# Queries and keys of a pair of heads: two transfers with a buffer each in place of one

## Chip, core and metric

The kernel runs on one NeuronCore of a Trainium2 chip. The metric is the device time of one execution in microseconds (us). Engines: PE multiplies matrices, DVE and ACT work on vectors, POOL hardly takes part, SP issues all transfers (DMAs).

## What is computed

Two parts, one after the other. First, attention over 8 batches of 8 heads (head dimension 64): 32 global tokens that see all 544 tokens, and 512 local tokens that see the global ones and a band of 32 to either side. Then a feed-forward layer on the 4352 tokens of 512 features. The reference, cut:

```python
def _attn_ref(q_l, k_l, v_l, q_g, k_g, v_g):
    s_g = scale * np.matmul(q_g, k_all.transpose(0, 1, 3, 2))
    out_g = np.matmul(sm(s_g), v_all)
    s_ll = np.where(np.abs(pos[:, None] - pos[None, :]) <= 32, scale * q_l @ k_l^T, -1e9)
    a_l = sm(np.concatenate([scale * q_l @ k_g^T, s_ll], axis=-1))
    out_l = np.matmul(a_l, np.concatenate([v_g, v_l], axis=2))
    return np.concatenate([out_g, out_l], axis=2)

def _moe_ref(x, w_in, w_out):          # x: all heads of a token side by side
    h = x @ w_in                        # 512 -> 2048
    sp = np.maximum(h, 0.0) + np.log1p(np.exp(-np.abs(h)))
    return (h * erf(sp)) @ w_out        # 2048 -> 512
```

All products are in float32: an operand is split into a high and a low part, and three products of parts are summed (names that end in h and l).

## The kernel before

**Attention.** The function `attention(b, h, key)` (line 480) records the operations of one head; heads come in pairs that share the loads of queries and keys. Of a pair, Q is 128 x 544 and K is 128 x 768 words (K holds the blocks of keys in the order in which the windows of 128 keys need them). From the second batch on both are one tensor `qk` in HBM and one buffer `QK` of two in the pool, with `View`s on the two parts (lines 489 to 491):

```python
QK = abuf([P, SQ + NENT * WB], f"qk_{nm}", "qk", 2)
Q, K = View(QK, lambda t: t[:, :SQ]), View(QK, lambda t: t[:, SQ:])
held_by = [QK]
```

and one load brings them (line 510). The first batch has separate buffers and loads already, in memory that serves the weights later (table `EARLY`, line 63). The scores `s` of a pair read Q and K; DVE masks them and finds maxima (`sm`, `mx`), ACT takes exponentials, PE transposes (`t`), ACT or DVE copies (`pt`), PE multiplies with the values `va` and `vb` (`o`), and the normalised rows go by `xn` and `xT` to a buffer `xsc` in HBM. The global tokens have the products `ga`, `gb`, `gt`, `go`, `gx`.

**Feed-forward.** A chunk is one batch of 512 local tokens; the ninth holds the global ones. Output weights are brought, converted on ACT and DVE and split (`raw_out`, `top_out`, `wouth`, `woutl`); three units of 256 features each are resident. Names such as `op_0_5_3` read: half 0 of the features, chunk 5, tile 3. For chunks 0 to 5 and 8, the first half is computed between the heads (`h`, then `sp`, `gh`, `gl`, then the projection `op`). The rest uses a two-level scheme with seven products for a pair of chunks (function `products`, line 1316; banks `pa`, `pb`, `pc`, `pd`), whose operands are blocks and sums of blocks of the chunks (function `pair_blocks`, line 1260; B11, T1, T2, B21, B22, T3, T4 from loads `rx`). The product pa needs B11, pb needs T2.

**The order of the work** is not written out. Every operation is recorded with the engines that may take it, an estimated duration and a key; `Program.schedule` (line 192) then plays the program through with a model of engines and transfers, takes at each moment the ready operation of the smallest key (products of one kind are kept together by `NEAR`), and the instructions are issued in the order it finds. SP's queue is one of the engines of that model, so all transfers stand in one order, and a transfer that waits for a buffer holds up those behind it. The keys come from some hundred numbers at the head of the file (`HKEYS`, `HOFF`, `QLEAD`, `WOUT`, `GA1` and others). In the views all operations have the lines of a few helpers: 398 and 399 for PE, 400 and 401 for ACT, 402 for transfers, 410 for DVE.

Of the kernel before, what the change touches and what calls it, by code (L numbers as in the profile page):

```python
# [12 lines left out]
F32 = mybir.dt.float32  # L13
# [9 lines left out]
P = 128  # L23
# [6 lines left out]
FIRSTU = 3  # L30
CROWD, STRETCH, EVADE = 254, 4.013, 0.444
LOADED = (8.0, 36.0, 5.5)
# [7 lines left out]
GOFF, POFF = 10.828, 3.328  # L40
WIN, WOUT = (4.562, -0.85, -2.097), (8.325, 8.046, 8.583)
BIASED, AG = 30, 3
SHARED = (-99.0, -3.776)
TPAIR = 4.07
KEEP, KSTEP, FIRST = 23.915, 0.995, (11.832, 24.33)
CVO = (28.333, 40.99, 63.455, 72.447, 78.297)
QLEAD2, XDEL, SLOTS = 4.703, -1.599, 11
GATE1, GATE2, PROJ1, PROJ2 = (23.641, 17.389, 19.913), (24.543, 35.77, 36.437), 20.101, 32.087
SPT = 0.35
BIAS, AHEAD = 1.451, 14.561  # L50

# [15 lines left out]
EARLY |= {f"vb_0_{h}": ("xh" if h % 2 == 0 else "xl", 3) for h in range(6)}  # L67
WLEAD = 2.692
LATER, GFIRST = 8, (-3.958, -8.992)
HOFF = (-0.395, -0.257, -0.438, -0.817, -0.264, -0.516, -0.398, -1.043, -0.725, 0.706, 1.098, 1.046, 1.486, -0.653, 2.583, -0.948, 0.685, -0.013, 0.188, 0.75, 0.727, 0.252, 0.107, -0.027, -0.444, -0.245, 0.179, 0.265, 4.756, -1.498, 3.211, 2.883)  # L70
XOFF = (11.098, -2.917, 1.105, 8.898, 3.5, -3.863, -28.764, 5.954, 2.659)
UOFF = (2.338, -0.165, -2.537, -3.201, 2.006, 5.153, 52.335, -8.177, -3.667)
GFF = (-1.126, -0.376, -2.083, -1.393, -3.192, -14.288, -5.04, -1.158, -9.133)
PFF = (-3.459, 0.743, -4.102, 3.348, 5.735, 1.295, -10.989, -6.661, 15.971)
KQ = (-1.903, 0.178, 5.248, 31.079, 26.846, -19.85, -36.139, 22.153, 100.464, 4.644)
NORMAL = 1.125 * 2.0**-15
STRAIGHT, XLATE = True, -0.456
NS = 1
CSLAG = -20.54
KIN = (15.525, 30.452, 26.054)  # L80
GA1, GA2, PA1, PA2 = (1.398, 1.139, 20.144), (20.415, 21.216), 12.862, 17.045
AOFF = (5.616, 3.312, -17.499, -6.93)
XDELA = (2.207, -33.316, -10.264, -7.382)
LOFF = (3.06, 3.64)
_TUNE = ("KIN", "GA1", "GA2", "PA1", "PA2", "AOFF", "XDELA", "LOFF", "CSLAG")
# [28 lines left out]
class View:


    def __init__(self, whole, cut):
        self.whole, self.cut = whole, cut

    @property  # L120
    def ap(self):
        return self.cut(self.whole.ap)

# [236 lines left out]
def kernel(  # L360
    ctx: ExitStack,
    tc: tile.TileContext,
    qk: bass.AP,
    vA: bass.AP,
# [6 lines left out]
    nc = tc.nc  # L371
    B, NPAIR, _, SQ = qk.shape
    SQ -= NENT * WB
    H = 2 * NPAIR
# [105 lines left out]
    def attention(b, h, key):  # L480
        nm = f"{b}_{h}"
        p, r0 = h // 2, (h % 2) * D
        if h % 2 == 0:
            parts = qk[b, p][:, :SQ], qk[b, p][:, SQ:]
            if f"k_{nm}" in EARLY:
                Q, K = abuf([P, SQ], f"q_{nm}", "q", 2), abuf([P, NENT * WB], f"k_{nm}", "k", 2)
                held_by = [Q, K]
            else:
                QK = abuf([P, SQ + NENT * WB], f"qk_{nm}", "qk", 2)
                Q, K = View(QK, lambda t: t[:, :SQ]), View(QK, lambda t: t[:, SQ:])  # L490
                held_by = [QK]
            st["now"] = Q, K, held_by
            if NH * b + h == 0:
                add({"SP": 0.01}, key - QLEAD - 0.01, lambda: None, [], [Q, K])
                for n, (q0, q1, k0, k1) in enumerate(((0, 288, 0, 416), (288, SQ, 416, NENT * WB))):
                    for j, (t, src, c0, c1) in enumerate(((Q, parts[0], q0, q1), (K, parts[1], k0, k1))):
                        PIECE[n, j] = fixed(None)
                        add(
                            {"SP": SPT},
                            key - QLEAD,  # L500
                            lambda t=t, src=src, c0=c0, c1=c1: dma(t.ap[:, c0:c1], src[:, c0:c1]),
                            [t],
                            [PIECE[n, j]],
                            moved=0.512 * (c1 - c0),
                        )
# [7 lines left out]
        (Q, K, held_by), XN = st["now"], st["xn"]  # L513
        VA = abuf([P, NENT // 4, D + 1], f"va_{nm}", "va", 5)
# [6 lines left out]
        if h % 2 == 0:  # L521
# [16 lines left out]
            if NH * b + h == 0:  # L538
                PIECE[2, 0] = fixed(None)
                for n in range(2):  # L540
                    need = [Q, K, PIECE[n, 0], PIECE[n, 1]]
                    add(
                        {"PE": 0.55},
                        key,
                        lambda n=n: scores(range(2 * n, 2 * n + 2)),
                        need + SS * n,
                        [PIECE[2, 0]] if n else SS,
                        heat=1024,
                        ins=64,
                        mode="S",  # L550
                    )
            elif h % 4 == 2 and b >= GSJOIN:
                GA, GB, more = global_scores(b, h // 4, [st["qk", 0], (Q, K, held_by)])
# [6 lines left out]
                add({"PE": 1.9}, key, joint, [*st["qk", 0][2], *held_by], [*SS, GA, GB, GTURN], heat=3136, ins=160, mode="S")  # L560
# [188 lines left out]
    def global_scores(b, j, qk):  # L749
# [817 lines left out]
```

## Time and profile before

| | us |
|---|---|
| median of 3 runs | 897.86 (897.18 to 898.85) |
| profiled execution | 901.88 |
| its span, first to last instruction | 900.1 |
| PE busy | 882.4 |
| DVE busy | 688.3 |
| ACT busy | 549.8 |
| mean granted clock of PE | 0.996 |

The page comes from one profiled execution. Its span runs from the first to the last instruction; the execution's own time is 1.78 us longer. A duration on PE is that of a matmul from its start to a modelled end, and matmuls overlap; the distance of two starts is the better price of one. An engine's idle time is charged to what ended it; "issue" means that the engine waited for nothing that the profile shows.

### The profile page before, as it was taken

What the parts mean: (1) busy time and instruction counts of PE and PEld (TensorE: products, weight loads), DVE (VectorE), ACT (ScalarE), POOL (GpSimd) and SP (SyncE); (2) the same over time, 40 slices, a digit from 0 to 9 for tenths busy, and PEclk for the clock granted to TensorE, in tenths of its full rate; (3) what the DMA queues carried; (4) which work ended last, traced back from release to release, by engine and by line L of the source; (5) the groups of instructions that cost most, each with busy time, mean ns of one, the idle gap of its engine ahead of it and who ended that gap; (6) DMA issues with size and microseconds to landing.
All of it is one profiled execution on the core that took longest, in us unless ns stands there. A gap on an engine that the chain in (4) does not pass through costs nothing.

```text
span 900.1 us, 22151 instructions
## 1 busy us (share of the span) xinstructions
PE 882.4 (98%) x8781; PEld 717.2 (80%) x8789; DVE 688.3 (76%) x1839; ACT 549.8 (61%) x948; POOL 0.9 (0%) x5
## 2 busy tenths in 40 slices
PE   8899899999999999999999999999999999999998
PEld 4677777777877888888888888888888888888986
DVE  6898998999999978978598987587555956456443
ACT  5588866885588746854564865456524654455660
POOL 0000000000000000000000000000000000000000
PEclk9999999999999999999999999999999999999999
DMA  9898798799788948368676528444393435435222
GB/s 322 293 294 293 267 301 301 257 306 320 265 273 286 313 132 281 105 239 277 213 249 202 178 69 269 164 119 151 108 279 102 134 114 176 146 93 171 75 78 70
DMA packets 120063, 186.43 MB, mean 207 GB/s; under 512 B 14104, under 2 KB 57624, under 8 KB 119960
## 3 DMA queue, kind: packets, MB, share of 16 engines
q1 hardware_dynamic: 119960, 185.02, 62.9%
q8 instruction: 69, 1.13, 0.5%
q14 instruction: 34, 0.28, 0.1%
HBM read 143.56 MB, written 41.42 MB: 206 GB/s over the span
## 4 chain that ended last, share of the span: by engine, by line
PE 88%; DVE 6%; DMA 2%; issue 2%; ACT 1%; SPq 1%; DVEq 0%; ACTq 0%
PE op L398 40%; PE h L398 10%; PE pd L398 7%; PE pc L398 7%; PE pa L398 7%; PE pb L398 3%; PE o L398 3%; PE t L399 3%; PE s L398 3%; DVE sm L410 2%; PE h_g L398 2%; PE gt L399 1%; PE go L398 1%; PE ga L398 1%; DMA k<-in_qk_dram 1%
## 5 line engine op out<-in xcount | busy, mean ns | idle before, releaser
L398 PE MATMUL op<-wouth,gh 128*128 128x512 f32 x544 | 214.8, 395 | 0.0
L398 PE MATMUL op<-wouth,gl 128*128 128x512 f32 x544 | 211.9, 390 | 0.0
L398 PE MATMUL op<-woutl,gh 128*128 128x512 f32 x544 | 211.9, 389 | 0.0
L401 ACT ACT_TABLE_LOAD x105 | 134.7, 1283 | 2.6 <-PEq L1554 0.7
L398 PEld LDWEIGHTS op<-wouth,gh 128*128 128x128 f32 x544 | 102.1, 188 | 21.5 <-issue 0.6
L398 PEld LDWEIGHTS op<-wouth,gl 128*128 128x128 f32 x544 | 102.1, 188 | 21.5
L398 PEld LDWEIGHTS op<-woutl,gh 128*128 128x128 f32 x544 | 102.2, 188 | 20.0
L410 DVE TENSOR_TENSOR gl<-sp,gh 128x512 fp32r<-128x512 f32 x136 | 91.2, 685 | 19.6 <-PE op L398 16.0
L400 ACT ACTIVATE gh<-sp 128x512 fp32r<-128x512 f32 x67 | 42.0, 631 | 100.7 <-PE op L398 91.4
L400 ACT ACTIVATE sp<-sp 128x512 f32<-128x512 f32 x136 | 76.0, 621 | 0.5
L410 DVE CAST gh<-sp 128x512 fp32r<-128x512 f32 x69 | 28.6, 421 | 55.3 <-PE op L398 54.9
L410 DVE CUSTOM_DVE_ANT_0 sm<-s,msk 128x128 f32<-128x128 f32 x256 | 57.1, 285 | 17.3 <-PE s L398 17.2
L398 PE MATMUL h<-xh,winh 128*128 128x512 f32 (+1 forms) x168 | 67.0, 399 | 0.0
L398 PE MATMUL pa<-xh_x_B,wq 128*128 128x512 f32 x184 | 63.9, 389 | 0.0
L398 PE MATMUL pd<-xh_ih_T,wq 128*128 128x512 f32 x184 | 63.8, 389 | 0.0
L398 PE MATMUL h<-xh,winl 128*128 128x512 f32 (+1 forms) x168 | 63.2, 376 | 0.0
L398 PE MATMUL h<-xl,winh 128*128 128x512 f32 (+1 forms) x168 | 63.1, 376 | 0.0
L410 DVE TENSOR_TENSOR pair<-u,pc 128x512 f32<-128x512 f32 x46 | 31.4, 683 | 32.9 <-PE pc L398 32.8
L400 ACT ACTIVATE sm<-sm,mx 128x128 f32<-128x128 f32 x120 | 37.4, 394 | 9.1 <-DVE mx L410 9.1
L399 PE MATMUL t<-cs,sm 128*128 128x128 f32 x256 | 39.2, 286 | 3.0 <-DVE rs L410 1.1
L398 PE MATMUL o<-va,pt 128*32 128x65 f32 x768 | 37.8, 222 | 4.2 <-issue 3.5
L400 ACT ACTIVATE pt<-t 128x512 f32<-128x512 f32 x52 | 30.0, 600 | 17.8 <-PE t L399 17.7
(160 smaller groups left out, 1687.9 us busy)
## 6 DMA issues: line engine op xcount, KB each, us to landing
wq<-wq SPq DMA_DIRECT2D x161, 256.0 KB, 3.4
vb<-in_vB_dram SPq DMA_DIRECT2D x64, 325.0 KB, 5.6
qk<-in_qk_dram SPq DMA_DIRECT2D x28, 656.0 KB, 5.9
rx<-xsc SPq DMA_DIRECT2D x26, 512.0 KB, 6.0
va<-in_vA_dram SPq DMA_DIRECT2D x64, 195.0 KB, 5.3
wq<-part SPq DMA_DIRECT2D x47, 256.0 KB, 4.5
part<-os SPq DMA_DIRECT2D x34, 256.0 KB, 3.3
os<-part SPq DMA_DIRECT2D x34, 256.0 KB, 4.2
```

What stands on the lines that cost most here:

```text
L398: pe = lambda n, *a, **k: pinned(nc.tensor.matmul(n, *a, **k))
L399: tr = lambda *a, **k: pinned(nc.tensor.transpose(*a, **k))
L400: act = lambda *a, **k: pinned(nc.scalar.activation(*a, **k))
L401: table = lambda name: pinned(nc.scalar.preload_act_table_set(name))
L410: return lambda *a, **k: pinned(f(*a, **k))
```

## The change

Queries and keys are two tensors in HBM (`qT`, `kE`). Every pair has a buffer Q and a buffer K, two of each in the pool, and two loads with the same key, queries first. The class `View` that cut a buffer in two is gone (a helper class that was called `Whole` now bears its name). The numbers that set the order have other values. The diff, cut (of the tables of numbers a few lines stand for all):

```diff
-CROWD, STRETCH, EVADE = 254, 4.013, 0.444
+CROWD, STRETCH, EVADE = 254, 4.013, 0.627
...
-HKEYS = ((0, -5.932), (11, -0.913), (22, 0.765), (64, 30.197))
-STEP, GKEY = 0.093, -1.339
-QLEAD, VLEAD, RLEAD, XLEAD = 0.027, -1.614, -0.422, 4.406
+HKEYS = ((0, -5.577), (11, -1.054), (22, 0.793), (64, 30.035))
+STEP, GKEY = 0.091, -1.319
+QLEAD, VLEAD, RLEAD, XLEAD = -0.05, -1.622, 0.29, 4.309
...
-NEAR = 3.364
+NEAR = 2.617
...
-            parts = qk[b, p][:, :SQ], qk[b, p][:, SQ:]
-            if f"k_{nm}" in EARLY:
-                Q, K = abuf([P, SQ], f"q_{nm}", "q", 2), abuf([P, NENT * WB], f"k_{nm}", "k", 2)
-                held_by = [Q, K]
-            else:
-                QK = abuf([P, SQ + NENT * WB], f"qk_{nm}", "qk", 2)
-                Q, K = View(QK, lambda t: t[:, :SQ]), View(QK, lambda t: t[:, SQ:])
-                held_by = [QK]
-            st["now"] = Q, K, held_by
+            st["q"] = Q = abuf([P, SQ], f"q_{nm}", "q", 2)
+            st["k"] = K = abuf([P, NENT * WB], f"k_{nm}", "k", 2)
...
-            elif len(held_by) == 2:
-                load(key - QLEAD, Q, parts[0], 278)
-                load(key - QLEAD, K, parts[1], 393)
             else:
-                load(key - QLEAD, QK, qk[b, p], 671)
-            st["qk", p % 2] = st["now"]
+                load(key - QLEAD, Q, qT[b, p], 278)
+                load(key - QLEAD, K, kE[b, p], 393)
+            st["qk", p % 2] = (Q, K)
...
-                add({"PE": 1.02}, key, scores, held_by, SS, heat=2048, ins=128, mode="S")
+                add({"PE": 1.02}, key, scores, [Q, K], SS, heat=2048, ins=128, mode="S")
...
-_INS = ["qk", "vA", "vB", "cst", "w_in", "w_out"]
+_INS = ["qT", "kE", "vA", "vB", "cst", "w_in", "w_out"]
...
-    return dict(qk=np.concatenate([qT, kE], axis=3), vA=vA, vB=vB, cst=cst, w_in=wi, w_out=wo)
+    return dict(qT=qT, kE=kE, vA=vA, vB=vB, cst=cst, w_in=wi, w_out=wo)
```

The order of the instructions moves with it. Three places follow, with the numbers of the buffers (the last number of a name only counts buffers; `qk_2_0` is the pair of heads 0 and 1 of batch 2).

SP, the loads of the first two pairs of batch 2, before:

```order
L402 DMA xsg_88<-gxT_1_0_1260 128x2x32
L402 DMA qk_2_0_1324<-in_qk_dram 128x1312
L402 DMA qk_2_2_1334<-in_qk_dram 128x1312
L402 DMA vb_1_7_1409<-in_vB_dram 128x650
L402 DMA vb_1_4_1424<-in_vB_dram 128x650
```

and in the changed kernel:

```order
L391 DMA xsg_88<-gxT_1_0_1268 128x2x32
L391 DMA q_2_0_1332<-in_qT_dram 128x544
L391 DMA k_2_0_1334<-in_kE_dram 128x768
L391 DMA q_2_2_1344<-in_qT_dram 128x544
L391 DMA k_2_2_1361<-in_kE_dram 128x768
L391 DMA vb_1_7_1421<-in_vB_dram 128x650
L391 DMA vb_1_4_1436<-in_vB_dram 128x650
```

Each load is cut in two, keys directly behind their queries, and the rest keeps its order. It is so for most pairs; in the whole program SP has 654 transfers in place of 626.

SP, the first two pairs of batch 3, before:

```order
L402 DMA qk_3_2_2058<-in_qk_dram 128x1312
L402 DMA xsc2_82<-xT_2_1_2032 128x512
L402 DMA qk_3_0_2076<-in_qk_dram 128x1312
L402 DMA vb_2_4_2133<-in_vB_dram 128x650
L402 DMA vb_2_5_2156<-in_vB_dram 128x650
L402 DMA va_2_7_2162<-in_vA_dram 128x390
L402 DMA va_3_2_2194<-in_vA_dram 128x390
```

and in the changed kernel:

```order
L391 DMA q_3_2_2074<-in_qT_dram 128x544
L391 DMA xsc2_82<-xT_2_1_2048 128x512
L391 DMA k_3_2_2092<-in_kE_dram 128x768
L391 DMA q_3_0_2139<-in_qT_dram 128x544
L391 DMA vb_2_4_2172<-in_vB_dram 128x650
L391 DMA vb_2_5_2178<-in_vB_dram 128x650
L391 DMA k_3_0_2189<-in_kE_dram 128x768
L391 DMA va_2_7_2196<-in_vA_dram 128x390
L391 DMA va_3_2_2221<-in_vA_dram 128x390
```

Here the keys come later than their queries: one store, or two loads of values, lie between.

PE, the hand-over from attention to the two-level products, where pa and pb of the first unit begin, before:

```order
L398 MATMUL op_0_5_3_7090<-woutl_0_1_1444,gh_0_5_3_7117 128x512
L398 MATMUL op_0_5_3_7090<-wouth_0_1_1079,gl_0_5_3_7132 128x512
L398 MATMUL pa_0_3_0_7226<-xh_x0_3_B11_7009,wq0_0_3_0_6788 128x512
L398 MATMUL pa_0_3_0_7226<-xl_x1_3_B11_7043,wq0_0_3_0_6788 128x512
L398 MATMUL pa_0_3_0_7226<-xh_x0_3_B11_7009,wq0_0_3_0_6788 128x512 x2
L398 MATMUL pa_0_3_0_7226<-xl_x1_3_B11_7043,wq0_0_3_0_6788 128x512
L398 MATMUL pa_0_3_0_7226<-xh_x0_3_B11_7009,wq0_0_3_0_6788 128x512
L398 MATMUL pb_0_3_0_7239<-xh_x2_3_T2_7129,wq4_0_3_0_6798 128x512
L398 MATMUL pb_0_3_0_7239<-xl_x3_3_T2_7155,wq4_0_3_0_6798 128x512
```

and in the changed kernel:

```order
L387 MATMUL op_0_4_3_7067<-woutl_0_1_2373,gh_0_4_3_6822 128x512
L387 MATMUL op_0_4_3_7067<-wouth_0_1_1933,gl_0_4_3_6829 128x512
L387 MATMUL pa_0_3_0_7111<-xh_x0_3_B11_7004,wq0_0_3_0_6839 128x512
L387 MATMUL pa_0_3_0_7111<-xl_x1_3_B11_7021,wq0_0_3_0_6839 128x512
L387 MATMUL pa_0_3_0_7111<-xh_x0_3_B11_7004,wq0_0_3_0_6839 128x512 x2
L387 MATMUL pa_0_3_0_7111<-xl_x1_3_B11_7021,wq0_0_3_0_6839 128x512
L387 MATMUL pa_0_3_0_7111<-xh_x0_3_B11_7004,wq0_0_3_0_6839 128x512
L387 MATMUL op_0_4_2_7041<-wouth_0_2_1085,gh_0_4_4_6737 128x512
L387 MATMUL op_0_4_2_7041<-woutl_0_2_1456,gh_0_4_4_6737 128x512
```

The product pa stood at row 2543 of PE's order and stands at 2471; behind it 24 projection matmuls of chunks 4 and 5 now come before pb, which followed it directly.

DVE at the same place, up to the low part of block T2, before:

```order
L410 TENSOR_TENSOR rt_0_3_7060<-rx_0_7_0_6884,rx_0_6_0_6862 128x1024
L410 TENSOR_TENSOR woutl_1_1_7034<-top_out_1_1_1_6978,wouth_1_1_6903 128x512
L410 TENSOR_TENSOR rx_0_7_0_6884<-rx_0_7_1_6931,rx_0_7_0_6884 128x1024
L410 TENSOR_TENSOR xl_il0_3_B22_7087<-rx_0_7_1_6931,xh_ih0_3_B22_7073 128x512 x2
L410 TENSOR_TENSOR xl_x7_3_T1_7100<-rt_0_3_7060,xh_x6_3_T1_7084 128x512 x2
L410 CAST gh_0_5_2_7112<-sp_0_5_2_6703 128x512
L410 TENSOR_TENSOR rt_0_3_7060<-rx_0_7_1_6931,rt_0_3_7060 128x1024
L410 TENSOR_TENSOR gl_0_5_2_7121<-sp_0_5_2_6703,gh_0_5_2_7112 128x512
L410 TENSOR_TENSOR gl_0_5_3_7132<-sp_0_5_3_6915,gh_0_5_3_7117 128x512
L410 TENSOR_TENSOR gl_0_5_4_7134<-sp_0_5_4_6916,gh_0_5_4_7114 128x512
L410 TENSOR_TENSOR gl_0_5_5_7153<-sp_0_5_5_6917,gh_0_5_5_7119 128x512
L410 TENSOR_TENSOR xl_x3_3_T2_7155<-rt_0_3_7060,xh_x2_3_T2_7129 128x512 x2
```

and in the changed kernel:

```order
L399 TENSOR_TENSOR gl_0_5_0_7106<-sp_0_5_0_6752,gh_0_5_0_7088 128x512
L399 TENSOR_TENSOR gl_0_5_2_7118<-sp_0_5_2_6754,gh_0_5_2_7090 128x512
L399 CAST gh_0_5_1_7120<-sp_0_5_1_6753 128x512
L399 TENSOR_TENSOR rt_0_3_7062<-rx_0_7_1_6951,rt_0_3_7062 128x1024
L399 TENSOR_TENSOR gl_0_5_1_7135<-sp_0_5_1_6753,gh_0_5_1_7120 128x512
L399 TENSOR_TENSOR gl_0_5_4_7146<-sp_0_5_4_6933,gh_0_5_4_7122 128x512
L399 TENSOR_TENSOR xl_x5_3_B21_7159<-rx_0_6_1_6953,xh_x4_3_B21_7108 128x512 x2
L399 CAST gh_0_5_3_7169<-sp_0_5_3_6932 128x512
L399 CAST gh_0_5_5_7171<-sp_0_5_5_6934 128x512
L399 TENSOR_TENSOR gl_0_5_3_7173<-sp_0_5_3_6932,gh_0_5_3_7169 128x512
L399 TENSOR_TENSOR gl_0_5_5_7182<-sp_0_5_5_6934,gh_0_5_5_7171 128x512
L399 TENSOR_TENSOR xl_x3_3_T2_7186<-rt_0_3_7062,xh_x2_3_T2_7137 128x512 x2
```

The conversion of the output weight (`woutl_1_1`) and block B22 no longer stand ahead of T2, and block B21 does. Further ahead, in rows not shown, the rest of that conversion (eight rows), a copy (`hs_0_5_5`) and, here, the cast `gh_0_5_2` have left, and copies (`os_0_3_2`, `os_0_4_0`, `os_0_4_1`, `hs_0_8_2`) and casts for blocks 8 and B11 have come, beside the two casts `gh` that are seen.

## Rows read from the trace of the kernel before

**Rows 1.** The page, busy time by engine (us, share of the span, instructions).

```profile
PE 882.4 (98%) x8781; PEld 717.2 (80%) x8789; DVE 688.3 (76%) x1839; ACT 549.8 (61%) x948; POOL 0.9 (0%) x5
```

**Rows 2.** Busy time by stretch: length, engines' busy us (count), PEclk, DMA share, GB/s.

```profile
29.98:33.39 3.41, 3.19 (x35) 2.54 (x38) 1.66 (x4) 2.02 (x6) 0.00 (x0) 0.50 1.05 406
98.24:101.65 3.41, 3.41 (x17) 3.41 (x18) 3.36 (x9) 1.50 (x4) 0.00 (x0) 0.50 1.02 396
101.65:235.00 133.35, 131.96 (x2495) 104.89 (x2493) 125.27 (x470) 97.11 (x186) 0.00 (x0) 1.00 0.86 283
235.00:346.00 111.00, 110.56 (x1768) 88.31 (x1761) 101.92 (x361) 77.20 (x138) 0.00 (x0) 1.00 0.75 250
346.00:896.20 550.20, 550.20 (x2518) 459.18 (x2516) 374.10 (x636) 303.87 (x446) 0.00 (x0) 1.00 0.51 162
```

**Rows 3.** Waits of PE, whole span: us in total, times, longest.

```profile
PE o L398 <- issue: 5.8, 6, 2.3
PE s L398 <- DMA k<-in_qk_dram: 1.4, 1, 1.4
```

**Rows 4.** Transfers, whole span: count, size, median us from issue to landing.

```profile
qk<-in_qk_dram SPq DMA_DIRECT2D x28, 656.0 KB, 5.9
k<-in_qk_dram SPq DMA_DIRECT2D x3, 384.0 KB, 5.9
q<-in_qk_dram SPq DMA_DIRECT2D x3, 272.0 KB, 5.4
```

**Rows 5.** The tile qk: ns of one issue (least/median/most), and landings.

```profile
L402 SPq DMA_DIRECT2D qk<-in_qk_dram x28: 327/333/1527, 19.3 to 305.8; - x28
DMA to landing us min/median/max: 4.1/5.9/8.5
```

**Rows 6.** Waits of SP's queue, 60 to 250 us, for earlier pairs.

```profile
SPq L402 <- DMA qk<-in_qk_dram: 3.2, 2, 1.6
```

**Rows 7.** Timeline, SP at 60 and PE at 66 us: start, us, what.

```profile
60.14 0.86 SPq L402 DMA_DIRECT2D qk<-in_qk_dram  x2
...
66.72 0.87 PE L398 MATMUL s<-qk 64*32 64x128 f32 x40
```

**Rows 8.** Timeline of PE at 225 us.

```profile
225.19 0.48 PE L398 MATMUL op<-wouth,gh 128*128 128x512 f32 x1
```

**Rows 9.** Timeline, DVE at 124 and PE at 132 us.

```profile
123.95 0.67 DVE L410 TENSOR_TENSOR woutl<-top_out,wouth 128x512 fp32r<-128x512 f32 x1
...
131.82 0.48 PE L398 MATMUL op<-wouth,gh 128*128 128x512 f32 x1
```

**Rows 10.** Chain of work that ended last: start, us, what.

```profile
371.78 16.35 PE op L398 x72
388.13 1.36 PE pa L398 x6
389.49 1.36 PE pb L398 x6
```

**Rows 11.** Timeline of DVE, 342 to 385 us, idle time in brackets.

```profile
342.92 0.75 DVE L410 CAST gh<-sp 128x512 fp32r<-128x512 f32 x2
...
356.18 0.69 DVE L410 SCALAR_TENSOR_TENSOR top_out<-wouth,top_out 128x512 f32<-128x512 f32 x1 [4.13 <-ACT wouth L400]
...
359.25 0.42 DVE L410 TENSOR_SCALAR top_out<-raw_out 128x512 int32<-128x512 int32 x1
...
359.70 1.42 DVE L410 SCALAR_TENSOR_TENSOR top_out<-raw_out,top_out 128x512 int32<-128x512 int32 x2
...
380.11 1.28 DVE L410 TENSOR_TENSOR xl_x_T<-rt,xh_x_T 128x512 fp32r<-128x512 f32 x2
...
384.85 0.68 DVE L410 COPY os<-op 128x512 f32<-128x512 f32 x1
```

**Rows 12.** Timeline of PE at 98 us; DMA queues, 94 to 97 us.

```profile
97.83 0.22 PE L398 MATMUL o<-vb,pt 128*32 128x65 f32 x1 [2.27 <-issue]
...
q8 instruction: 1, 0.02, 2.5%
```

More of the change, by code (lines that the diff above doesn't have):

```diff
@@ L35 @@
 SPARE = 120.0
-HKEYS = ((0, -5.932), (11, -0.913), (22, 0.765), (64, 30.197))
-STEP, GKEY = 0.093, -1.339
-QLEAD, VLEAD, RLEAD, XLEAD = 0.027, -1.614, -0.422, 4.406
-GOFF, POFF = 10.828, 3.328
-WIN, WOUT = (4.562, -0.85, -2.097), (8.325, 8.046, 8.583)
-BIASED, AG = 30, 3
[L43 to L48, printed above, removed]
+HKEYS = ((0, -5.577), (11, -1.054), (22, 0.793), (64, 30.035))
+STEP, GKEY = 0.091, -1.319
+QLEAD, VLEAD, RLEAD, XLEAD = -0.05, -1.622, 0.29, 4.309
+GOFF, POFF = 10.903, 3.269
+WIN, WOUT = (5.497, -0.591, -2.036), (7.878, 7.976, 7.683)
+BIASED, AG = 30, 3
+SHARED = (-99.0, -6.134)
+TPAIR = 4.162
+KEEP, KSTEP, FIRST = 24.202, 0.997, (14.919, 21.808)
+CVO = (29.418, 49.586, 62.202, 70.69, 78.568)
+QLEAD2, XDEL, SLOTS = 3.736, -2.127, 11
+GATE1, GATE2, PROJ1, PROJ2 = (23.21, 19.728, 20.256), (23.691, 34.482, 29.13), 20.389, 28.848
 SPT = 0.35
-BIAS, AHEAD = 1.451, 14.561
+BIAS, AHEAD = 1.425, 14.731
 MORE = {"vb": 2}
@@ L67 @@
 EARLY |= {f"vb_0_{h}": ("xh" if h % 2 == 0 else "xl", 3) for h in range(6)}
[L68 to L75, printed above, removed]
+WLEAD = 2.867
+LATER, GFIRST = 8, (-3.614, -8.715)
+HOFF = (-0.45, -0.475, -0.269, -0.647, -0.188, -0.482, -0.45, -1.01, -0.908, 0.737, 0.684, 0.98, 1.743, -0.774, 2.64, -0.296, 0.828, 0.15, 0.264, 0.626, 0.527, 0.063, 0.095, 0.02, -0.309, -0.553, -0.02, 0.389, 4.956, -0.868, 2.871, 3.597)
+XOFF = (13.185, -3.269, 1.253, 9.043, 3.338, -5.698, -31.909, 3.776, -4.386)
+UOFF = (2.523, -0.341, 0.508, -3.401, 1.274, 3.537, 49.801, -5.105, -6.263)
+GFF = (-1.093, -0.108, -1.726, -1.34, -3.335, -13.307, -3.45, -1.541, -9.084)
+PFF = (-3.097, 0.98, -4.418, 3.818, 5.316, 4.779, -7.042, -4.564, 17.933)
+KQ = (-1.999, 0.271, 5.281, 25.186, 29.01, -15.289, -31.313, 21.094, 98.134, 1.26)
 NORMAL = 1.125 * 2.0**-15
-STRAIGHT, XLATE = True, -0.456
+STRAIGHT, XLATE = True, -0.377
 NS = 1
[L79 to L84, printed above, removed]
+CSLAG = -20.903
+KIN = (15.308, 31.147, 26.266)
+GA1, GA2, PA1, PA2 = (7.892, 4.021, 27.993), (20.854, 19.58), 10.028, 16.739
+AOFF = (4.197, -0.882, -18.129, -9.016)
+XDELA = (0.843, -37.222, -9.568, -4.456)
+LOFF = (5.155, 4.837)
 _TUNE = ("KIN", "GA1", "GA2", "PA1", "PA2", "AOFF", "XDELA", "LOFF", "CSLAG")
@@ L111, in __init__ @@
         self.writers, self.readers = [], []
[L114 to L122, printed above, removed]
 class Part:
@@ L362 @@
     tc: tile.TileContext,
-    qk: bass.AP,
+    qT: bass.AP,
+    kE: bass.AP,
     vA: bass.AP,
@@ L371 @@
     nc = tc.nc
-    B, NPAIR, _, SQ = qk.shape
-    SQ -= NENT * WB
+    B, NPAIR, _, SQ = qT.shape
     H = 2 * NPAIR
@@ L495, in attention @@
                 for n, (q0, q1, k0, k1) in enumerate(((0, 288, 0, 416), (288, SQ, 416, NENT * WB))):
-                    for j, (t, src, c0, c1) in enumerate(((Q, parts[0], q0, q1), (K, parts[1], k0, k1))):
+                    for j, (t, src, c0, c1) in enumerate(((Q, qT, q0, q1), (K, kE, k0, k1))):
                         PIECE[n, j] = fixed(None)
@@ L505, in attention @@
                         )
-            elif len(held_by) == 2:
-                load(key - QLEAD, Q, parts[0], 278)
-                load(key - QLEAD, K, parts[1], 393)
-            else:
-                load(key - QLEAD, QK, qk[b, p], 671)
-            st["qk", p % 2] = st["now"]
+            else:
+                load(key - QLEAD, Q, qT[b, p], 278)
+                load(key - QLEAD, K, kE[b, p], 393)
+            st["qk", p % 2] = (Q, K)
             st["xn"] = abuf([P, 4, P], f"xn_{nm}", "xn", 2)
-        (Q, K, held_by), XN = st["now"], st["xn"]
+        Q, K, XN = st["q"], st["k"], st["xn"]
         VA = abuf([P, NENT // 4, D + 1], f"va_{nm}", "va", 5)
@@ L552, in attention @@
             elif h % 4 == 2 and b >= GSJOIN:
-                GA, GB, more = global_scores(b, h // 4, [st["qk", 0], (Q, K, held_by)])
+                GA, GB, more = global_scores(b, h // 4, [st["qk", 0], (Q, K)])
                 G0[b, h // 4] = GA, GB
@@ L908, in split @@
         )
-    class Whole:
+    class View:
         def __init__(self, buf, f=lambda a: a):
@@ L917, in load_w @@
     def load_w(key, src, name, HI, LO, i, deps, lead):
-        TOP = Whole(mbuf([P, 512], F32, f"top_{name}", ("wt", "wr")[i % 2], 1))
-        H, L = (Whole(b, lambda a: a[:, i, :]) for b in (HI, LO))
+        TOP = View(mbuf([P, 512], F32, f"top_{name}", ("wt", "wr")[i % 2], 1))
+        H, L = (View(b, lambda a: a[:, i, :]) for b in (HI, LO))
         to_fp32(key, src, name, TOP, H, deps, lead)
```

16 lines of the change are left out of this document (8 added, 8 removed).

## The prediction

> **What bounds the kernel now.** I read the page's busy times first, then the busy times by stretch, then the waits of PE, then the transfers. PE is busy for 882.4 of 900.1 us [rows 1]. The stretches show what kind of bound that is: from 346.0 to 896.2 us PE is busy in every one of 550.20 us, with DVE at 374.10 and ACT at 303.87 beside it, so nothing there can be won, and only a new wait can be added; from 101.65 to 235 us PE lacks 1.39 us, and from 235 to 346 us 0.44 us [rows 2]. All that is idle before that lies in the first 102 us and the largest part of it is not a wait for data: the view of waits has 5.8 us in six gaps before the products of attention (o) that it puts to "issue", and a single wait for queries or keys, 1.4 us in the first batch [rows 3], which the change leaves alone. Two stretches of 3.41 us run at a granted clock of 0.50, the 1.2 GHz level, and PE works through 3.19 and 3.41 us of them; at 2.4 GHz that work would take half, so the clock costs 1.6 + 1.7 us. Of the 17.7 us in which PE is not busy, 1.39 and 0.44 lie in those two stretches, so 15.9 us, most of them in the first 102 us, and 3.3 us of clock are all that can be won; what can be lost has no such bound.
>
> The profiled execution took 901.88 us, of which 900.1 are the span. The median of the unprofiled runs is 897.86, 4.0 less. I form the sum as a difference to the profiled execution and carry the difference over to the median.
>
> **The change, part by part.** *The transfers.* 28 loads of 656 KB become 28 of 272 and 28 of 384 KB; the first batch was split already. The bytes stay, so the engines that move them gain or lose only what smaller transfers cost. The trace has all three sizes: from issue to landing 5.9 us for the whole, 5.9 us for keys alone and 5.4 us for queries alone [rows 4]. Landing hardly depends on size here, so two that follow each other land one issue apart: 0.33 us, the duration of an issue [rows 5]. The Trainium skill ("DMA: Bandwidth & Descriptors", Rules for kernel authors) speaks against the change: it wants small transfers joined and at least 1 MiB per transfer for full bandwidth, and its section on the anatomy of a DMA gives a fixed cost of about 2.0 us for one, though for the other issuing path; 28 such costs one after the other would be 56 us by estimate, while the rows show them overlapped.
>
> *SP.* 28 more issues at 0.33 us are 9.2 us of the SP queue, spread from 19.3 to 305.8 us [rows 5]. SP is not on the path; what pays is the load that stands behind. As the order of SP shows, the keys stand directly behind their queries in most places, so all later loads move by 0.33 us. SP also waits now and then until an earlier transfer has landed: for qk 3.2 us in two waits, the longest 1.6, between 60 and 250 us [rows 6]. More transfers in flight can make that more frequent. Which load has no room for it? The tightest pair is the first of batch 2: issued at 60.14 us, its first score product starts at 66.72, 6.58 us later [rows 7], against landings of 4.1 to 8.5, median 5.9 [rows 5]. With the keys 0.33 us later the median landing is at 66.4: still covered, by 0.3 us. With the longest landing the product starts at 69.0, 2.3 us late. I take 0.3 us, near the median, and keep 0 and 2.3 as ends. No gain can come from here, since a product needs both buffers and both are released by the same readers.
>
> *The order of the work.* The amounts do not change: each kind of matmul has the same count on PE, and so have the 47 filler products. The first 1529 of 4661 rows of PE's order are the same but for the names of the buffers; the first that moves is a projection product that starts at 225.19 us now [rows 8]. So in the first 225 us only the timing of transfers can move PE. One thing there does change place: units 1 and 2 of the output weights swap their loads and conversions. Unit 2 is ready now at 123.95 + 0.67 = 124.6 us, and the first product with unit 1 starts at 131.82 [rows 9]; converted last, unit 1 is there 7.2 us early. Cost 0, and a delay of over 7.2 us would be needed to make one.
>
> *The hand-over from attention to the two-level products.* Here PE's order changes by an amount that the trace prices. Now 72 projection matmuls, 16.35 us from 371.78 to 388.13, stand directly ahead of the first product pa; in the changed order pa is 72 rows earlier, so it would start at 371.78. The second one, pb, starts at 389.49 now [rows 10]. In the changed order it follows pa (1.36 us) and 24 matmuls (24 x 16.35/72 = 5.45 us): 378.6 us. It needs the block T2, which DVE finishes now at 380.11 + 1.28 = 381.4 [rows 11], 8.1 us early. To meet 378.6, DVE must come 2.8 us sooner. Its order does that: between the last attention tile and T2 it drops the conversion of an output weight (two times 0.42 + 1.42 + 0.68 + 0.68, and a cast of 0.42; durations as in [rows 11], where equal shapes take about the same), block B22 (1.28), a copy (0.68) and a cast (0.42), 9.2 us; it takes up three copies (2.04; one of them only moves across the start of the count, so 1.36), a copy of 0.68, casts of 0.42, 0.75 and 0.75, and B21 (1.28), 5.2 us. That is 4.0 us less: T2 at 377.4, a margin of 1.2 us where there were 8.1. The 4.13 us that DVE stands idle there for ACT [rows 11] can shrink or grow: without it T2 is at 373.3; with 4.13 more at 381.5, 2.9 us late. I take 0.3 us, close to the margin, ends 0 and 2.9.
>
> *The rest, 390 to 896 us*, has the same pattern of products and projections with a few groups exchanged. PE never waits there, beside a DVE that is idle for a third of the time [rows 2]. I take 0; a gain is excluded, since PE has no gap to fill.
>
> Sum: 0.3 + 0 + 0.3 + 0 = +0.6 us, so 902.5 for a profiled execution and **898.5** for the median.
>
> **The rivals.** A measurement of this kernel tells about 0.2%, 1.8 us, from no change.
>
> A, the forecast: loads stay covered and the hand-over just holds. 898.5; its own range goes from 897.2, the fastest run shown with both terms at 0, to 899.6, the border of no change.
>
> B, slower: DVE is late with T2 or with a later block, since the margin shrinks from 8.1 to 1.2 us. The place is pb; it decides once DVE is idle over 1.2 us more than now. One more idle stretch of 4.13 us gives 2.9 us beyond the margin: 897.86 + 0.6 + 2.9 = 901.4. Against it: the order of DVE was arranged for the earlier product. For it: the margin is smaller than one wait for ACT.
>
> C, slower: queries or keys land late. In a stretch where transfers keep the queue full, a pair costs more than one, and PE waits at the first pair of batch 2, from the point at which landing takes over 6.2 us. Price 2.3 us: 900.5 with the other term. For it: the longest landing is 8.5 us; against it: the other pairs have far more room, and queries alone landed in 5.4. The Trainium skill's rule on joining small transfers, named above, is this rival.
>
> D, faster: the largest gap, 2.27 us before an o product at 97.83, is charged to "issue", and in the 3 us around it the queue that brings instructions moved a packet [rows 12]; right behind it, at 98.24, the clock falls to 0.50 for 3.41 us. The Trainium skill ("Runtime: NRT & Kernel Launch", Instruction fetch mechanics) says that a sequencer refills its instructions by its own DMA queue in 16 KiB blocks. SP's order changes just there, with the two pairs of batch 3 cut into four pieces; if the block comes sooner the gap and the slow clock both go: -2.27 - 1.7 + 0.6, so 894.5. Against it: the bytes ahead of it hardly change, so the gap can as well grow.
>
> That the change doesn't do what it says can't be: the order shows 654 transfers where there were 626, and two buffers per pair.
>
> **How the numbers follow.** A 0.47: the larger part of the program is unchanged and the rest has no gap. B 0.22, C 0.14, D 0.17. Faster by over 0.2% is D, 0.17; within it A, 0.47; slower B and C, 0.36. The range reaches above to 902.0, which takes in B and C and their small terms together up to 4 us, and below to 896.0, half of D; what is left out is about half of D and a tenth above.
>
> **What would show it.** Right: PE busy without a gap from 346 us on, the first pa within 2 us of 371.8, no wait of PE for q or k beyond the first batch, gaps before o products of 4 to 8 us in all, two stretches at clock 0.50. Wrong: a wait for q or k before s of batch 2 (C), a wait of pb or pc for a block (B), one or no stretch at 0.50 (D), or a wait of op products behind 400 us, which no term here has.

## The result and the profile after

The forecast of 898.5 us was wrong: the changed kernel takes **905.52 us** (median of 4 runs, 903.53 to 906.43) where the kernel before takes 898.36 in the same comparison (4 runs, 897.18 to 899.68). The ratio is 1.0076, 95% interval 1.0053 to 1.0100, so 4.8 to 9.0 us slower, outside the range and on the other side of the 0.2%. Executions of one and the same kernel lie up to 7 us apart here (29 of the kernel before went from 896.39 to 903.72, median 899.02), and a profile shows one of them: that of before was a long one (901.88), that of after the shortest of its four (903.53).

The page of after, busy time by engine, answers to [rows 1]:

```profile
PE 880.8 (98%) x8781; PEld 715.7 (79%) x8789; DVE 688.2 (76%) x1831; ACT 555.9 (62%) x954; POOL 0.9 (0%) x5
```

The same number of matmuls, and PE is busy 1.6 us less. Busy time by stretch of after, columns as in [rows 2]: length, busy us (count) of PE, PEld, DVE, ACT, POOL, then PEclk, DMA share, GB/s:

```profile
101.65:235.00 133.35, 131.62 (x2465) 105.15 (x2449) 126.16 (x478) 93.67 (x176) 0.00 (x0) 1.00 0.88 291
235.00:346.00 111.00, 110.81 (x1758) 88.77 (x1757) 100.72 (x354) 77.04 (x135) 0.00 (x0) 1.00 0.72 235
346.00:893.64 547.64, 547.64 (x2506) 456.96 (x2505) 372.51 (x623) 310.17 (x456) 0.00 (x0) 1.00 0.51 162
...
893.64:901.70 8.06, 0.00 (x0) 0.00 (x0) 0.76 (x2) 0.00 (x0) 0.00 (x0) 0.66 0.40 124
```

and the stretch behind the last matmul of before, which no row ahead of the prediction showed:

```profile
896.29:900.10 3.81, 0.00 (x0) 0.00 (x0) 0.76 (x2) 0.00 (x0) 0.00 (x0) 1.00 0.39 138
```

This is the larger part of the surprise, 4.2 us of some 6.8. PE has no gap from 346 us on, as before, and it is done at 893.64 us, **2.65 us earlier** than in the profile of before (one execution of each). Then 8.06 us pass until the end, where 3.81 passed. In that time DVE works for 0.76 us in both; what is left is the landing of the last stores.

Waits of PE in after, whole span (us in total, times, longest), answering to [rows 3]:

```profile
PE o L387 <- issue: 2.4, 4, 1.6
PE s L387 <- issue: 2.1, 4, 0.9
PE x L388 <- issue: 1.9, 1, 1.9
PE o L387 <- DMA vb<-in_vB_dram: 1.2, 1, 1.2
...
PE s L387 <- DMA k<-in_kE_dram: 0.7, 1, 0.7
```

No wait for q or k is in the list beyond the 0.7 us of the first batch. The 1.2 us for values (vb), at 14.7 us, is a wait that before does not have; of the other profiles with the new numbers only one, of the numbers alone, has its like, so that it doesn't account for what is left over below. The transfers of after (count, KB, median us from issue to landing), answering to [rows 4]:

```profile
k<-in_kE_dram SPq DMA_DIRECT2D x31, 384.0 KB, 5.1
q<-in_qT_dram SPq DMA_DIRECT2D x31, 272.0 KB, 4.5
```

Each piece lands sooner than the 5.9 us of the whole. The hand-over, answering to [rows 10, 11]: the chain of waits of after (start, us, what), then DVE's and PE's timeline at T2 and pb.

```profile
365.05 4.11 PE op L387 x18
369.16 1.36 PE pa L387 x6
370.52 5.44 PE op L387 x24
375.96 1.36 PE pa L387 x6
377.32 2.72 PE op L387 x12
380.04 1.36 PE pb L387 x6
```

```profile
375.33 1.29 DVE L399 TENSOR_TENSOR xl_x_T<-rt,xh_x_T 128x512 fp32r<-128x512 f32 x2
```

```profile
379.88 0.39 PE L387 MATMUL pb<-xh_x_T,wq 128*128 128x512 f32 x1
```

T2 is ready at 375.33 + 1.29 = 376.62 and pb starts at 379.88: 3.3 us of margin, and no wait. The rows of PE's order ahead of the prediction stopped short here: behind the 24 projections comes a second group of pa, then 12 more projections, and only then pb.

Now the end. SP's issues of the last stores in before (start, us of the issue):

```profile
886.16 0.69 SPq L402 DMA_DIRECT2D out_dram<-os  x1
887.52 0.55 SPq L402 DMA_DIRECT2D out_dram<-os  x1
892.97 0.34 SPq L402 DMA_DIRECT2D out_dram<-os  x1
894.32 0.34 SPq L402 DMA_DIRECT2D out_dram<-os  x1
895.69 0.33 SPq L402 DMA_DIRECT2D out_dram<-os  x1
896.78 0.33 SPq L402 DMA_DIRECT2D out_dram<-os  x1
897.20 0.38 SPq L402 DMA_DIRECT2D out_dram<-os  x1
```

and in after, from the first store of chunk 8 on:

```profile
890.32 0.70 SPq L391 DMA_DIRECT2D out_dram<-os  x1
891.67 0.54 SPq L391 DMA_DIRECT2D out_dram<-os  x1
893.04 0.34 SPq L391 DMA_DIRECT2D out_dram<-os  x1
894.13 0.34 SPq L391 DMA_DIRECT2D out_dram<-os  x1
894.56 0.91 SPq L391 DMA_DIRECT2D out_dram<-os  x1
```

The two long issues (0.69 and 0.55, 0.70 and 0.54 us) are the two tiles of chunk 8: each goes to 4 separate pieces of 32 rows of the output (line 1134 of the changed kernel). In before they leave 5.5 us ahead of the next store, which is that of the first tile of chunk 5; in after they come in the middle of chunk 5, 1.4 us ahead of its third tile. (Chunk 5 has four tiles, the last stored in two halves.) What that does is seen in the time from issue to landing (least, median, most) of the ordinary stores in these stretches, in before and in after:

```profile
DMA to landing us min/median/max: 1.7/2.0/2.6
```

```profile
DMA to landing us min/median/max: 5.9/6.0/6.7
```

SP's closing waits in the trace of after say the same: it waits until 896.55 us for the first store of chunk 8 (6.2 us after its issue) and until 899.12 for the second (7.5), and the ordinary ones behind them are there at 899.74, 900.09 and 900.42. How fast such a store is can be read in before, in a stretch in which nothing else moves:

```profile
890.00:892.97 2.97, 2.97 (x15) 2.45 (x14) 0.69 (x1) 0.00 (x0) 0.00 (x0) 1.00 0.26 101
```

0.26 of 16 engines are 4.2 engines, at 101 GB/s. In after the same rate comes back behind PE's end, when the other engines have nothing left to move:

```profile
897.50:898.50 1.00, 0.00 (x0) 0.00 (x0) 0.00 (x0) 0.00 (x0) 0.00 (x0) 0.50 0.26 100
```

The Trainium skill ("DMA: Bandwidth & Descriptors", Why a DMA increments its semaphore by 16 and not by 1) says that the number of engines is the largest one up to 16 that divides the slowest dimensions of both sides of a transfer, here 128 partitions and 4 pieces, so 4: the trace agrees, with 4.2.

### The profile page after: what moved, and what is told of

Same layout as the page of the kernel before. It is cut to its first block, busy times and chain, and to the rows that moved or that the text cites. A ratio compares the mean times of both kernels' runs of the same rounds, so it can differ in the third digit from the quotient of the medians.

```text
span 901.7 us, 22181 instructions
## 1 busy us (share of the span) xinstructions
PE 880.8 (98%) x8781; PEld 715.7 (79%) x8789; DVE 688.2 (76%) x1831; ACT 555.9 (62%) x954; POOL 0.9 (0%) x5
## 4 chain that ended last, share of the span: by engine, by line
PE 92%; DVE 3%; DMA 1%; issue 1%; SPq 1%; ACT 1%; DVEq 0%; ACTq 0%
PE op L387 41%; PE h L387 11%; PE pd L387 7%; PE pc L387 7%; PE pa L387 7%; PE pb L387 3%; PE s L387 3%; PE o L387 3%; PE t L388 3%; PE h_g L387 2%; DVE sm L399 1%; PE ga L387 1%; PE go L387 1%; PE gt L388 1%; DMA k<-in_kE_dram 1%
## 5 line engine op out<-in xcount | busy, mean ns | idle before, releaser
L389 ACT ACTIVATE gh<-sp 128x512 fp32r<-128x512 f32 x73 | 46.2, 633 | 135.8 <-PE op L387 129.5
L399 DVE CAST gh<-sp 128x512 fp32r<-128x512 f32 x63 | 26.2, 421 | 33.9 <-PE op L387 33.9
L387 PE MATMUL s<-k,q 64*32 64x128 f32 x2048 | 40.1, 274 | 2.8 <-issue 2.1
L387 PEld LDWEIGHTS pd<-xh_ih_T,wq 128*128 128x128 f32 x184 | 34.5, 188 | 7.2
L387 PEld LDWEIGHTS pa<-xh_x_B,wq 128*128 128x128 f32 x184 | 34.5, 188 | 7.2
```

The costliest lines, as they stand in the source:

```text
L387: pe = lambda n, *a, **k: pinned(nc.tensor.matmul(n, *a, **k))
L389: act = lambda *a, **k: pinned(nc.scalar.activation(*a, **k))
L399: return lambda *a, **k: pinned(f(*a, **k))
```

## The experiments

**Theory T:** the time is lost behind the last matmul, because the new numbers issue the stores of chunk 8 late and those behind them land after them. **Rival S:** the split itself costs. The first two runs take the change apart.

*The split alone*: the changed code, and in it the lines 29 to 84 of before.

```diff
-GATE1, GATE2, PROJ1, PROJ2 = (23.21, 19.728, 20.256), (23.691, 34.482, 29.13), 20.389, 28.848
+GATE1, GATE2, PROJ1, PROJ2 = (23.641, 17.389, 19.913), (24.543, 35.77, 36.437), 20.101, 32.087
...
-LOFF = (5.155, 4.837)
+LOFF = (3.06, 3.64)
```

> The split alone: separate tensors, buffers and loads, with the numbers that set the order as before the change. PE's order is then the one of before, row for row at the end of the program. Theory T (the time was lost behind the last matmul: the two stores of chunk 8, which the new numbers issue last, hold up the stores behind them): within 1.5 us of the kernel before (898.4), with some 3.8 us from the last matmul to the end. Rival S (the split costs, by more transfers or later keys): 901.5 to 905.5, with idle time of PE before scores.

Measured: 901.65 us, ratio 1.0026 (1.0008 to 1.0043), 3.56 us behind the last matmul. In between: as a time it lies at the lower end of S (901.5 to 905.5), as a difference it is 2.3 us where S, set against 898.4, meant 3.1 or more; T allowed 1.5. T explains the larger part of the change's time only if the second run shows it.

*The numbers alone*: the code of before with the changed lines 29 to 84.

> The numbers alone: one transfer for queries and keys as before, with the numbers of the changed kernel. Theory T: as the changed kernel, 905.5 within 1.5 us, with 8 us from the last matmul to the end. Rival S: as the kernel before, 898 to 900.

Measured: 904.71 us, 1.0062 (1.0039 to 1.0085), and behind the last matmul:

```profile
895.58:903.49 7.91, 0.00 (x0) 0.00 (x0) 0.76 (x2) 0.00 (x0) 0.00 (x0) 0.67 0.40 125
```

The numbers alone make the long end and most of the time. Next, the end by itself. *The stores of chunk 8 cut in four*, nothing else moved, in the changed kernel, in the one before, and in the one with the numbers alone:

```diff
-dma(out_rows(c, t)[..., cols], O.ap[:, cols])
+for j in range(4):                       # chunk 8 only
+    n = (4 * t + j) * SQ
+    dma(out[n : n + SG, cols], O.ap[SG * j : SG * j + SG, cols])
```

> The changed kernel with each of the two stores of chunk 8 (4 x 32 rows) issued as four stores of 32 rows, at the same place of the order; nothing else moves. Theory T (a store whose outermost dimension is 4 is carried by few DMA engines, and the last stores land behind it): the time behind the last matmul falls from 8.1 to about 4 us, so 905.5 - 4.1 = 901.4. Rival M (the last stores are late for another reason, such as the amount of data at the end): 905.5 within 1 us, still 7 to 8 us behind the last matmul.

Measured: 901.94 us, 1.0032 (1.0016 to 1.0048), against 1.0076 whole. The end of the changed kernel with cut stores:

```profile
899.96:904.30 4.34, 0.00 (x0) 0.00 (x0) 0.76 (x2) 0.00 (x0) 0.00 (x0) 1.00 0.50 161
```

It falls from 8.06 to 4.34 us, as T wants (this profile was the longest of its 12 runs, 906.08). M is out.

> The kernel before with the same cut of the two stores. There they are issued at 886.2 and 887.5 us, five us ahead of the next store. Theory T: at most 0.6 us (the first ordinary store landed 2.6 us after its issue where the next took 2.0), so 898.4 to 897.8, no difference that the measurement tells. Rival M: the same, or slower by the six added issues (6 x 0.34 = 2.0 us of SP) if SP is what ends last: 900.4.

Measured: 900.87 us, 1.0010 (0.9991 to 1.0029): no difference that can be told, as both expected; 3.67 us behind the last matmul. With four stores the engines are busier while chunk 8 leaves, 0.53 in place of 0.26:

```profile
885.00:888.00 3.00, 3.00 (x15) 2.49 (x14) 0.14 (x1) 0.00 (x0) 0.00 (x0) 1.00 0.53 136
```

> The numbers of the changed kernel, one transfer for queries and keys as before, and the stores of chunk 8 cut in four: only the split is missing against the changed kernel with cut stores (901.9). Theory U (behind the stores, the split itself costs some 2.5 us, as it did alone, 901.65 against 899.0): 899 to 900. Rival N (the rest is the new order, and the split costs nothing): 901.0 to 902.0.

Measured: 900.76 us, 1.0018 (1.0006 to 1.0031), between the two; against the 1.0032 with the split the intervals overlap. It shows that the numbers cost something beside the long end, and doesn't tell U from N.

*The stores of chunk 8 late in the kernel before*: two instructions of SP's queue change place, nothing on another engine.

```diff
...
-for op in prog.schedule():
+order = prog.schedule()
+glob = [op for op in order if op in GSTORE]     # the two stores of chunk 8
+last = [op for op in order if op in LSTORE]     # the five of chunk 5
+for op in glob:
+    order.remove(op)
+at = order.index(last[1]) + 1
+order[at:at] = glob
+for op in order:
```

> The kernel before, with nothing changed but the place of the two stores of chunk 8 in SP's queue: behind the second store of chunk 5, where the changed kernel has them, in place of ahead of the first. They are then issued at about 894.7 and 895.1 us and not at 886.2 and 887.5. Theory T: the time from the last matmul to the end grows from 3.8 to 8 us or more, as in the changed kernel: 899.0 + 4.2 = 903.2, up to 904.5 since here the stores come after, not ahead of, most of the last products. Rival M (the stores don't hold up the others): 899.0 within 1 us.

Measured: 905.87 us, 1.0068 (1.0056 to 1.0080), more than expected. Its end:

```profile
894.16:904.18 10.02, 0.00 (x0) 0.00 (x0) 0.76 (x2) 0.00 (x0) 0.00 (x0) 0.70 0.40 103
```

10.02 us in place of 3.81 are 6.2 us, and the ratio is worth 6.1. This is the cleanest run of the study: the place of two stores makes the kernel before as slow as the changed one. A part of the excess over the expectation is that the second store leaves 0.8 us ahead of the last matmul's end (893.32 and 894.16), where it left 2.0 ahead in after.

*Two numbers of the changed kernel as before* (the keys of a projection and of the last unit), so that chunk 8 comes ahead of chunk 5 again:

```diff
-GATE1, GATE2, PROJ1, PROJ2 = (23.21, 19.728, 20.256), (23.691, 34.482, 29.13), 20.389, 28.848
+GATE1, GATE2, PROJ1, PROJ2 = (23.21, 19.728, 20.256), (23.691, 34.482, 29.13), 20.389, 32.087
...
-LOFF = (5.155, 4.837)
+LOFF = (3.06, 3.64)
```

> The changed kernel with two of its numbers as before: the key of the second projection of a pair of chunks (28.848 back to 32.087) and those of the last unit. The stores of chunk 8 are then issued ahead of chunk 5's again, whole as they are. Theory T: the time behind the last matmul falls from 8.1 to some 3.8 us, 901.4 as with cut stores (901.9). Rival M (it is not the order of the stores): 904.5 or more.

Measured: 904.18 us, 1.0059 (1.0043 to 1.0075): a miss, and only just short of M's 904.5. The order was as intended, the time was not:

```profile
889.32 0.69 SPq L391 DMA_DIRECT2D out_dram<-os  x1
890.68 0.55 SPq L391 DMA_DIRECT2D out_dram<-os  x1
```

```profile
895.36:901.65 6.29, 0.00 (x0) 0.00 (x0) 0.76 (x2) 0.00 (x0) 0.00 (x0) 0.68 0.45 149
```

The stores lead, but only by 1.4 us over the next one at 892.03, which landed at 898.73, 0.6 us after 890.68 + 7.5. So it is not the order that counts but the distance: some 7.5 us from the second of these stores to its landing must pass ahead of the end. Here it left 4.7 us ahead of PE's end (895.36 - 890.68) in place of 2.0, and the end shrank from 8.06 to 6.29. Even in before, with 5.5 us between, the first store behind the two landed 2.6 us after its issue, where the next took 2.0.

**What the split costs.** Five runs ask for the 2.3 us that the split alone took.

*Each load of q and of k in two halves by columns* (split alone; the first batch's loads too, all but the first pair, so 90 added transfers over before where the split adds 28, and not the 84 of the expectation):

```diff
-load(key - QLEAD, Q, qT[b, p], 278)
-load(key - QLEAD, K, kE[b, p], 393)
+for t, src, n, kbytes in ((Q, qT[b, p], SQ, 278), (K, kE[b, p], NENT * WB, 393)):
+    def halves(t=t, src=src, n=n):
+        for c in (slice(0, n // 2), slice(n // 2, n)):
+            dma(t.ap[:, c], src[:, c])
+    add({"SP": SPT}, key - QLEAD, halves, writes=[t], moved=kbytes)
```

> The split alone, with the numbers of before, but each load of queries and each of keys issued as two transfers of half the columns: 56 transfers more than with two. PE's order is the one of before. Theory U (each added transfer costs, in the queue or on the engines): 28 added transfers cost 2.6 us, 84 cost 7.9, so 899.0 + 7.9 = 906.9; at least 904. Rival V (the 2.6 us are not a price per transfer but where the blocks of PE's instructions happen to land): 899.0 to 902.5.

Measured: 903.90 us, 1.0053 (1.0034 to 1.0072). It is more than V allows, and less than U's sum (for 90, 8.4 us over before where 4.8 were measured), just under its floor: neither holds as put.

*One tensor and one buffer, two transfers* in the kernel before:

```diff
-load(key - QLEAD, QK, qk[b, p], 671)
+dma(QK.ap[:, :SQ], src[:, :SQ])
+dma(QK.ap[:, SQ:], src[:, SQ:])
```

> The kernel before, one tensor and one buffer for queries and keys, but brought by two transfers of 272 and 384 KB issued one behind the other. Theory U (it is the added transfers that cost in the split): 899.4 + 2.6 = 902.0. Rival W (it is the separate buffers, which let keys come later than their queries): 899.4 within 1 us.

Measured: 900.37 us, 1.0009 (0.9999 to 1.0020): inside W's range, and the interval leaves out U's 902.0; a smaller cost of the added transfers stays possible (-0.1 to 1.8 us).

The other three use the gaps charged to "issue". *64 matmuls of 8 columns ahead of the program*:

```diff
+for _ in range(64):
+    pe(spare[:, :8], warm[:, :P], warm[:, :8], start=True, stop=True)
 for op in prog.schedule():
```

> The kernel before with 64 matmuls of 8 columns ahead of everything, whose results nobody reads, while PE waits for its first data anyway. They move every later instruction of PE by 128 places. Theory F (gaps charged to issue are waits for the next 16 KB block of PE's instructions, 256 of them): the gaps stay at instructions 185 to 189 of a block, counted from the start, so they come at other operations than now: none at 68.61, 73.74, 97.83 and 147.57 us, where they end before, but 128 instructions ahead or behind. The time moves either way by up to 3 us. Rival G (the gaps belong to the operations, by a wait that the trace doesn't show): the gaps stay at the same products s and o, and the time is 899.0 within 1 us.

Measured: 897.71 us, 0.9984 (0.9969 to 0.9999). PE's timeline of the kernel before, its gaps over 0.3 us charged to issue between 60 and 150 us:

```profile
68.61 0.53 PE L398 MATMUL s<-qk 64*32 64x128 f32 x20 [1.02 <-issue]
...
73.74 0.24 PE L398 MATMUL o<-va,pt 128*32 128x65 f32 x1 [0.66 <-issue]
...
97.83 0.22 PE L398 MATMUL o<-vb,pt 128*32 128x65 f32 x1 [2.27 <-issue]
...
147.57 0.22 PE L398 MATMUL o<-va,pt 128*32 128x65 f32 x1 [0.71 <-issue]
```

and the same with the 64 matmuls ahead:

```profile
66.19 0.24 PE L398 MATMUL o<-va,pt 128*32 128x65 f32 x1 [1.87 <-issue]
...
90.01 0.25 PE L398 MATMUL o<-vb,pt 128*32 128x65 f32 x2 [0.43 <-issue]
...
97.63 0.55 PE L399 MATMUL t<-cs,sm 128*128 128x128 f32 x3 [2.07 <-issue]
```

Counting PE's weight loads and matmuls from the start of the trace tells what these places are:

| kernel | gap ends, us | number in PE's records | remainder by 256 | packet of the instruction queue landed |
|---|---|---|---|---|
| before | 68.61 | 2746 | 186 | 67.34 |
| before | 73.74 | 3002 | 186 | 72.28 |
| before | 97.83 | 4025 | 185 | 96.56 |
| before | 147.57 | 5817 | 185 | 146.09 |
| 64 ahead | 66.19 | 2745 | 185 | 64.93 |
| 64 ahead | 90.01 | 3768 | 184 | 88.73 |
| 64 ahead | 97.63 | 4025 | 185 | 96.05 |

The operations change (the large gap is at a transposition t where it was at an o), the remainder stays, and each gap ends 1.3 to 1.6 us after a 16 KB packet of the queue that carries instructions has landed. The packets count with the blocks: 10 of that queue have landed ahead of the gap at record 2746 (10 x 256 + 186), 22 ahead of that at 5817 (22 x 256 + 185). So it is with each of the 99 such gaps over 0.3 us in the 14 profiles of this case, with 1.2 to 1.6 us from landing to end. Theory F holds: PE waits there for its next 256 instructions.

> The kernel before with 32 such matmuls, which move PE's instructions by 64 places. Theory F (the gaps are waits for blocks of 256 instructions): the gaps stay at instruction 185 of a block, at other operations than in both kernels so far; which time this gives depends on the operations that the borders meet, 896 to 901. Rival G: 899.4 within 0.5, with the gaps of before.

Measured: 900.32 us, 1.0001 (0.9990 to 1.0013). The gaps are again one remainder, at other places (38.30 at go, 68.09 and 85.38 at s); the remainder is 193 to 194 in this trace, and in every trace of the same batch, which has all 47 filler matmuls on record where the trace of before has 39.

> The split with the numbers of before, and the 64 matmuls of 8 columns ahead that move PE's instructions by 128 places. Against the shifted kernel with one transfer (897.7). Theory U (the split delays every block of instructions, wherever its border lies): 897.7 + 2.6 = 900.3. Rival X (the split's 2.6 us belong to the borders as they lay): 897 to 898.5.

Measured: 898.90 us, 0.9995 (0.9979 to 1.0011), against 0.9984 of the shifted kernel without the split: 1.0 us apart, between U and X, and inside both intervals.

**The sum of the runs.** Over before: the ratio less one, times the median of before in that comparison (898 to 900). End: from the last matmul to the end in the profile. Rest: what is over when the end's excess over 3.81 is taken off.

| kernel | over before, us | end, us | rest, us |
|---|---|---|---|
| changed | 6.8 | 8.06 | 2.6 |
| numbers alone | 5.6 | 7.91 | 1.5 |
| split alone | 2.3 | 3.56 | 2.6 |
| changed, cut stores | 2.9 | 4.34 | 2.4 |
| numbers alone, cut stores | 1.6 | 4.23 | 1.2 |
| before, stores late | 6.1 | 10.02 | -0.1 |
| changed, two keys as before | 5.3 | 6.29 | 2.8 |

The end is 4.2 of 6.8 us, taken from one profiled execution of each kernel. Of the rest, the split takes 2.6 us with the old numbers, 1.1 with the new (2.6 - 1.5), 1.2 with cut stores (2.4 - 1.2): always a loss, but only the first is clear of nothing by its interval (0.7 to 3.9 us over before); the others are not, at some 1.5 us to either side; the other 1.2 to 1.5 us come with the numbers. Where on the chip these two small parts arise stays open: the gaps at instruction blocks could be the place, since those over 0.2 us sum up to anything from 6.3 to 11.9 us in the 14 profiles, but with so large a spread these do not show whether the split makes them larger.

## Why the prediction was wrong

**The step that failed** is the last one: "The rest, 390 to 896 us ... I take 0; a gain is excluded, since PE has no gap to fill." Its reading of PE was right (547.64 of 547.64 us busy). Its fault was to stop at 896, where PE stops: the 3.81 us behind belonged to no term of the sum; they stand, unnoticed, in the 15.9 us of idle time that the prediction put for the most part into the first 102 us. A few groups of products were exchanged among each other at the end, at no cost to PE, and the second of the two stores that hang on chunk 8 went from 8.8 us ahead of PE's end (896.29 - 887.52) to 2.0 (893.64 - 891.67). Behind the first, it needs 7.5 us to land. The term should have been: 891.67 + 7.5 for the second store, three more landings of 0.3 to 0.6 us and 1.3 us to close, 901.7 as the end of the span: 4.2 us more than before. With it the forecast would have been 898.5 + 4.2 = 902.7, already above the range. What is left from there to 905.5 is about the rest of the table (2.6 us), whose place is not known. The Trainium skill ("DMA: Bandwidth & Descriptors", Rules for kernel authors) warns of an outermost dimension under 16; the prediction cited the same table for joining small transfers and passed this rule over, and it bore on the larger part.

*Transfers, +0.3.* Low in size, and the mechanism is open. No wait for q or k appeared; the first pair of batch 2 had its keys issued at 59.05 us and its first product at 65.51, 6.5 us for a landing of 5.1. Yet the split cost 1 to 2.6 us in the runs, near the end of 2.3 that was kept, and not through the wait that C names; only the run of the split alone (0.7 to 3.9) is clear of the 0.3.

*SP, 9.2 us more of issues:* off the path, as said.

*w_out swap, 0:* no wait of PE names an output weight at that place. Right.

*Hand-over, +0.3.* It held: no wait, 3.3 us of margin for the 1.2 worked out. The first pa came at 369.2, 2.6 us ahead of the forecast and outside its 2 us. T2 came 0.8 us sooner than forecast (376.6 for 377.4), and pb later (379.9 for 378.6), since the second group of pa and the 12 more projections stand ahead of it.

*Rivals.* B and C did not happen. D's clock did, as chance: the profile of after has no stretch at 0.50 before PE is done, that of before two, and PE finished earlier by 2.65 us; D's cause, that instruction packets make the gaps, is now shown. By the prediction's own sign (one or no stretch at 0.50) this should have meant a faster kernel, and it was a slower one: the sign told of PE and not of the end. But the gaps and the clock differ between profiles of one and the same order of PE: the kernel before with late stores has no stretch at 0.50 ahead of PE's end either, and its gaps at the borders sum to 8.9 us where before has 7.2. So this gain is not one of the changed kernel.

## What to carry to other kernels

Where PE is busy to its last matmul, price what follows it: list the last stores in the queue's order, and for each its issue plus its own landing time, since an end that no engine works in does not show in any busy share. A store whose outermost dimension is small is to leave early or to be cut so that more DMA engines carry it (0.53 of the 16 busy in place of 0.26); here cutting two stores in four was worth some 4 us (1.0076 to 1.0032) to a kernel that issues them late, and nothing that could be told to one that issues them early. And when a table of numbers moves everything at once, the ends of the program are the places where order is not free.

## What the runs showed that was not expected

The gaps charged to "issue" in attention are waits for PE's instructions. Those over 0.3 us come at a border of 256 instructions, at few of the some 69 borders of an execution, and end 1.2 to 1.6 us after the packet has landed; in the kernel before they make up most of the 5.8 us before o [rows 3]. The Trainium skill ("Runtime: NRT & Kernel Launch", Instruction fetch mechanics) has the 256 instructions, which the trace confirms, and calls the cost of a border mostly hidden. By the count of borders that holds here; the ones that show cost up to 2.3 us each in before, all of them in attention, where small matmuls run at a pace of 40 in 0.87 us [rows 7] and loads keep the DMA engines busy. That these two are the reason was not tested.

Whether the place of the borders is worth something by itself is not shown. With 64 small matmuls ahead the kernel before ran at 0.9984 (0.9969 to 0.9999), the one version here that beats both, and with 32 at 1.0001. The first interval hardly leaves out 1 and is one of thirteen; the 64 matmuls also change what PE does at the start; and the gaps in the profile of that kernel (one of its longest executions) sum to 10.0 us, where before has 7.2. At most it is luck of position and not a rule, and both kept the spread from one execution to the next.
